# The whole attention in 64-row matmuls that run in pairs on the two halves of the array

## The chip, the cores and the metric

The kernel runs on one core of one Trainium2 chip. The metric is the device time of one execution in microseconds, the median over the runs shown. TensorE (PE) does the matmuls and, in rows marked PEld, loads their weights; VectorE (DVE), ScalarE (ACT) and GpSimd (POOL) do the elementwise work; SyncE (SP) issues nearly all transfers.

## The reference

Three layers follow one another on u, v of shape (4, 3072, 256) and z of shape (4, 3072, 64), in fp32:

```python
scores = (1.0 / S) * np.matmul(z, z.transpose(0, 2, 1))      # S = 3072, 64 columns of z
attn = np.maximum(scores, 0.0) ** 2
x = u * np.matmul(attn, v)                                   # attention
k = np.maximum(xk @ w_k, 0.0); r = sigmoid(xr @ w_r)         # channel mix, xk and xr mix x with x shifted by a row
x = r * (k * k @ w_v)
out = np.maximum(x @ w_in, 0.0) ** 2 @ w_out                 # mlp, 256 -> 2048 -> 256
```

## The kernel before, in words

Every fp32 value is held as two fp32r parts, a high part and a low part (`hi` and `lo`: `lo` is the value minus `hi`), and a product is the sum of hi by hi, lo by hi and hi by lo. So an ordinary product costs three matmuls of 128 rows by 128 columns by 512 columns of moving data.

**Order.** All instructions stand in program order on each engine (`tc.manual_schedule()`, line 823): first `attention`, then `channel_mix`, then `mlp`. Each engine works its own list strictly in that order.

**Attention.** There are 4 batches of 6 blocks (`NBLK` = 24), each block holding 512 rows of the output, transposed (two halves d = 0, 1 of 128 features). A block is made of 24 chunks (`NJ`) of 128 keys; one chunk is one step `s` of the loop in lines 493 to 502. In a step the things planned for it in `todo` come first (loads, the preparation of z, v and u, conversions of weights, the gate of the block before), then `scores` of a chunk that lies up to 7 steps ahead (`LEAD`), then `attend` of chunk s.

`scores` (lines 340 to 361) computes a tile of 128 keys by 512 rows. The scores of a batch are symmetric, so a tile below the diagonal (`g < ib`) is not computed: it was turned on DVE when its mirror image was made (`turn`, line 318), stored to DRAM, and is read back (`load_turned_scores`, line 329), after which ACT makes `hi` (line 346) and DVE `lo` (line 347). Block `ib` of a batch therefore computes 24 - 4 ib chunks and reads 4 ib. For a computed chunk, z with its 64 columns fills the 128 rows of the array with two parts: `zhl` holds hi in rows 0 to 63 and lo in rows 64 to 127, `zlh` the other way round. Two matmuls of 128 rows (lines 351 and 352) give all four products hi·hi + lo·lo and lo·hi + hi·lo. ACT then does relu from PSUM (line 162) and square (line 163), ACT or DVE makes `hi` (lines 356 and 358), DVE turns it where needed (line 322) and makes `lo` (line 361). The score banks are four (`ps_w`), one for each chunk.

`attend` (lines 370 to 383) adds a chunk into the two accumulators of the block (d = 0, 1) with six matmuls: v hi by hi and v lo by hi for each d (lines 379 and 380), then v hi by lo for each d (line 383). The accumulators of odd and even blocks are different banks (`ps_a`, `ps_v`), two each, so eight banks are in use with the four of the scores.

`gate` (lines 385 to 389) is planned for the first step of the next block: for each d one DVE multiplication of the accumulator (in PSUM) by u, then a transfer to DRAM.

**The channel mix of block 0** (`up1` and `down1`, eight times six matmuls each) is spread over steps of the last attention block (lines 474 to 478); the rest, for blocks 1 to 23, is in `channel_mix`.

## Time and profile before

| | |
|---|---|
| median of 3 runs | 2537.62 us (2537.33 to 2539.25) |
| profiled execution | 2538.36 us, span of its instructions 2536.6 us |
| PE busy | 2513.0 us (99%), 11040 matmuls |
| PEld busy | 2072.7 us (82%), 11040 weight loads |
| DVE, ACT, POOL busy | 2007.8 (79%), 1664.6 (66%), 0.2 us (0%) |
| mean granted TensorE clock | 0.998 |

The page of the profile gives the share of the span in which each engine was busy, the chain of work that ended last, and groups of instructions by source line. The views by window give the same for a stretch of the span; timelines list instructions in order, with the idle time before them in square brackets and what released them. A matmul's duration there (0.39 us) is from its start until its result stands, and the next one starts before that; the distance of two starts is what it costs.

### The profile page before, as it was taken

How to read it: one execution, taken by the hardware profiler on the slowest of the kernel's cores; microseconds unless marked ns; L12 is line 12 of the kernel's file. 1: busy time of each engine (PE TensorE's matmuls, PEld its weight loads, DVE VectorE, ACT ScalarE, POOL GpSimd, SP SyncE). 2: the span in 40 equal slices, each digit the busy share in tenths (PEclk: the TensorE clock that was granted, in tenths of full speed). 3: DMA queues.
4: the chain of work that ended last, by engine and by line, in shares of the span. 5: the costliest groups of instructions: out<-in, count | busy, mean ns of one | idle time of the engine just before them, and what ended most of it. 6: DMA issues, size and time to landing. Idle time of an engine off the chain costs nothing.

```text
span 2536.6 us, 31670 instructions
## 1 busy us (share of the span) xinstructions
PE 2513.0 (99%) x11040; PEld 2072.7 (82%) x11040; DVE 2007.8 (79%) x3382; ACT 1664.6 (66%) x2879; POOL 0.2 (0%) x4
## 2 busy tenths in 40 slices
PE   7999999999999999999999999999999999999998
PEld 5888888888888888888888888788888888888887
DVE  8898988988988986777776677877777777777776
ACT  8766876786687654555555566666666666666665
POOL 0000000000000000000000000000000000000000
PEclk9999999999999999999999999999999999999999
DMA  7678677787886770111111112100110011100101
GB/s 189 173 201 202 195 200 186 201 229 185 198 232 185 211 188 26 58 59 42 59 34 50 47 54 67 28 23 17 34 34 17 17 34 34 26 26 17 34 17 17
DMA packets 311121, 243.79 MB, mean 96 GB/s; under 512 B 211377, under 2 KB 229809, under 8 KB 307889
## 3 DMA queue, kind: packets, MB, share of 16 engines
q1 hardware_dynamic: 308848, 241.25, 35.6%
q8 instruction: 86, 1.41, 0.2%
q10 hardware_dynamic: 2112, 0.52, 0.1%
q14 instruction: 75, 0.61, 0.1%
HBM read 136.86 MB, written 104.86 MB: 95 GB/s over the span
## 4 chain that ended last, share of the span: by engine, by line
PE 92%; DVE 3%; ACT 2%; DMA 1%; issue 1%; SPq 1%; DVEq 0%; ACTq 0%
PE ups L652 16%; PE ups L208 13%; PE v L379 9%; PE v L383 9%; PE v L380 9%; PE v L668 6%; PE v L669 6%; PE v L670 6%; PE v L234 3%; PE v L230 3%; PE v L231 3%; PE sps L352 3%; PE sps L351 3%; DMA mixed<-turned 1%; ACT s L692 0%
## 5 line engine op out<-in xcount | busy, mean ns | idle before, releaser
L380 PE MATMUL v<-ahi,vhl 128*128 128x512 f32 x1152 | 448.8, 390 | 2.6 <-DVE vhl L286 2.6
L379 PE MATMUL v<-ahi,vhl 128*128 128x512 f32 x1152 | 449.1, 390 | 1.1 <-ACT ahi L346 1.1
L689 ACT ACTIVATE s<-s 128x512 f32<-128x512 f32 x288 | 181.2, 629 | 333.5 <-DVE s L684 333.4
L383 PE MATMUL v<-alo,vhl 128*128 128x512 f32 x1152 | 356.1, 390 | 4.0 <-DVE alo L361 3.9
L163 ACT ACTIVATE a<-a 128x512 f32<-128x512 f32 x528 | 333.9, 632 | 16.8
L652 PE MATMUL ups<-d,win 128*128 128x512 f32 x1152 | 323.7, 389 | 0.0
L668 PE MATMUL v<-hhi,wout 128*128 128x512 f32 x768 | 299.3, 390 | 0.7 <-ACT hhi L697 0.6
L670 PE MATMUL v<-hlo,wout 128*128 128x512 f32 x768 | 299.3, 390 | 0.5 <-DVE hlo L703 0.5
L669 PE MATMUL v<-hhi,wout 128*128 128x512 f32 x768 | 298.8, 389 | 0.0
L208 PE MATMUL ups<-mixed,wk 128*128 128x512 f32 x1152 | 291.8, 389 | 0.0
L703 DVE TENSOR_TENSOR hlo<-s,hhi 128x512 fp32r<-128x512 f32 x384 | 264.6, 689 | 21.7 <-ACT hhi L697 9.5
L162 ACT ACTIVATE a<-ups 128x512 f32<-128x512 f32 x192 | 114.8, 598 | 235.9 <-PE ups L208 207.9
L383 PEld LDWEIGHTS v<-alo,vhl 128*128 128x128 f32 x1152 | 215.5, 188 | 52.3 <-DVE alo L361 7.9
L380 PEld LDWEIGHTS v<-ahi,vhl 128*128 128x128 f32 x1152 | 216.6, 188 | 48.3 <-DVE vhl L286 3.4
L379 PEld LDWEIGHTS v<-ahi,vhl 128*128 128x128 f32 x1152 | 216.7, 188 | 47.1 <-ACT ahi L346 2.0
L652 PEld LDWEIGHTS ups<-d,win 128*128 128x128 f32 x1152 | 216.3, 188 | 44.9
L208 PEld LDWEIGHTS ups<-mixed,wk 128*128 128x128 f32 x1152 | 216.2, 188 | 44.9
L162 ACT ACTIVATE a<-sps 128x512 f32<-128x512 f32 x336 | 199.2, 593 | 81.5 <-PE sps L352 73.7
L652 PE MATMUL ups<-b,win 128*128 128x512 f32 x864 | 242.9, 389 | 0.0
L692 ACT ACTIVATE s<-s 128x512 f32<-128x512 f32 x384 | 231.2, 627 | 6.1
L322 DVE STREAM_TRANSPOSE turn<-a 128x512 f32<-128x512 f32 x240 | 207.2, 864 | 18.3 <-ACT a L163 16.8
L361 DVE TENSOR_TENSOR alo<-a,ahi 128x512 fp32r<-128x512 f32 x336 | 220.3, 660 | 0.0
(103 smaller groups left out, 3918.0 us busy)
## 6 DMA issues: line engine op xcount, KB each, us to landing
turned<-turn SPq DMA_DIRECT2D x60, 1024.0 KB, 5.1
mixed<-turned SPq DMA_DIRECT2D x220, 256.0 KB, 5.4
raw<-in_v_dram SPq DMA_DIRECT2D x24, 512.0 KB, 4.7
u<-in_u_dram SPq DMA_DIRECT2D x192, 64.0 KB, 4.3
xT<-uT SPq DMA_DIRECT2D x48, 256.0 KB, 2.2
x2d<-xo SPq DMA_DIRECT2D x48, 256.0 KB, 2.2
x<-x2d SPq DMA_DIRECT2D x12, 1024.0 KB, 4.8
out_dram<-y SPq DMA_DIRECT2D x92, 128.0 KB, 2.9
```

The source lines that it names most:

```text
L162: nc.scalar.activation(out=a, in_=ps, func=AF.Relu, scale=scale)
L163: nc.scalar.activation(out=a, in_=a, func=AF.Square)
L208: nc.tensor.matmul(ps, lhsT=lhs(h, c, f), rhs=rhs[:, m, c, :], start=k == 0, stop=k == 3 * ND - 1)
L379: nc.tensor.matmul(acc[n][d], lhsT=vt[:, 0, c, ds_], rhs=hi, start=first, stop=False)
L380: nc.tensor.matmul(acc[n][d], lhsT=vt[:, 1, c, ds_], rhs=hi, start=False, stop=False)
L383: nc.tensor.matmul(acc[n][d], lhsT=vt[:, 0, c, ds_], rhs=lo, start=False, stop=last)
L652: nc.tensor.matmul(ps, lhsT=win[q][:, h, r, w], rhs=x(y), start=first and m == 0, stop=m == 2, skip_group_check=not first)
L668: nc.tensor.matmul(acc[p, b][d], lhsT=w[:, 0, c, ds_], rhs=hi, start=first, stop=False)
L669: nc.tensor.matmul(acc[p, b][d], lhsT=w[:, 1, c, ds_], rhs=hi, start=False, stop=False)
L670: nc.tensor.matmul(acc[p, b][d], lhsT=w[:, 0, c, ds_], rhs=lo, start=False, stop=last)
L692: nc.scalar.activation(out=tmp[g, c], in_=tmp[g, c], func=AF.Square)
L703: nc.vector.tensor_tensor(out=lo, in0=tmp.pop((g, c)), in1=hi, op=ALU.subtract)
```

## The change

In the attention every matmul of 128 rows becomes two of 64 rows, one on rows 0 to 63 and one on rows 64 to 127 of the array, issued one right after the other into PSUM banks of their own.

- Scores are made for two chunks at once (at an even chunk): three products hi·lo, hi·hi, lo·hi of 64 rows each, chunk c on the upper half of the rows and chunk c + 1 on the lower. The product lo·lo is not computed any more. Two banks hold the pair (`ps_s`); both relus are issued together, square and the rest follow chunk by chunk.
- In `attend` each product of 128 keys becomes two of 64 keys, into two accumulators. A block has four accumulators; those of d = 0 exist twice (`bufs=2`, four banks), those of d = 1 once (two banks).
- At the end of a block `gate` adds the halves: for each d an ACT copy of the second half out of PSUM, then for d = 0 a DVE addition from PSUM, for d = 1 a DVE copy of the first half out of PSUM and a POOL addition; the multiplication by u is POOL's.
- At the start of a block the order is: chunk 0 for d = 0, chunk 1 for d = 0, then chunk 0 for d = 1, then chunk 1 for d = 1.
- The channel mix of block 0 is taken out of the last attention block and done at the start of `channel_mix`, whose PSUM pools are now opened after the attention.

```diff
-    ps_v = ctx.enter_context(tc.tile_pool(name="ps_v", bufs=1, space=PSUM))
-    ps_a = ctx.enter_context(tc.tile_pool(name="ps_a", bufs=1, space=PSUM))
-    ps_w = ctx.enter_context(tc.tile_pool(name="ps_w", bufs=4, space=PSUM))
...
+    HALVES = slice(0, P // 2), slice(P // 2, P)
...
+            ps_s = st.enter_context(tc.tile_pool(name="ps_s", bufs=2, space=PSUM))
+            ps_d = [st.enter_context(tc.tile_pool(name=f"ps_{d}", bufs=ND - d, space=PSUM)) for d in range(ND)]
...
-                cs = slice(c * P, (c + 1) * P)
-                ps = ps_w.tile([P, T], F32, tag="w", name="sps")
-                nc.tensor.matmul(ps, lhsT=zhl[b, g][:, cs], rhs=zhl[b, ib], start=True, stop=False)
-                nc.tensor.matmul(ps, lhsT=zlh[b, g][:, cs], rhs=zhl[b, ib], start=False, stop=True)
-                a = relu2(ps, 1.0 / S)
+                if c % 2 == 0:
+                    ps = [ps_s.tile([P, T], F32, tag="w", name="sps") for _ in HALVES]
+                    for k in range(3):
+                        for i, rows in enumerate(HALVES):
+                            top, low = (zlh, zhl) if i else (zhl, zlh)
+                            nc.tensor.matmul(ps[i], lhsT=(low, top, top)[k][b, g][rows, (c + i) * P:(c + i + 1) * P],
+                                             rhs=(top, low, top)[k][b, ib][rows], start=k == 0, stop=k == 2)
+                    for i in range(2):
+                        rel[s + i] = t = el.tile([P, T], F32, tag="a", name="a")
+                        nc.scalar.activation(out=t, in_=ps[i], func=AF.Relu, scale=1.0 / S)
+                a = rel.pop(s)
+                nc.scalar.activation(out=a, in_=a, func=AF.Square)
...
-            def attend(s):
+            def attend(s, d, terms):
+
                 n, b, ib, g, c = chunk(s)
                 first, last = s % NJ == 0, s % NJ == NJ - 1
-                if first:
-                    acc[n] = acc_tiles(ps_a if n % 2 else ps_v)
-                hi, lo = at.pop(s)
-                vt = vhl[b, g]
-                for d in range(ND):
-                    ds_ = slice(d * P, (d + 1) * P)
-                    nc.tensor.matmul(acc[n][d], lhsT=vt[:, 0, c, ds_], rhs=hi, start=first, stop=False)
-                    nc.tensor.matmul(acc[n][d], lhsT=vt[:, 1, c, ds_], rhs=hi, start=False, stop=False)
-                for d in range(ND):
-                    ds_ = slice(d * P, (d + 1) * P)
-                    nc.tensor.matmul(acc[n][d], lhsT=vt[:, 0, c, ds_], rhs=lo, start=False, stop=last)
+                if first and terms[0] == 0:
+                    acc[n, d] = [ps_d[d].tile([P, T], F32, tag=f"r{i}", name=f"v{d}") for i in range(2)]
+                vt, ds_ = vhl[b, g], slice(d * P, (d + 1) * P)
+                for k in terms:
+                    for i, rows in enumerate(HALVES):
+                        nc.tensor.matmul(acc[n, d][i], lhsT=vt[rows, k % 2, c, ds_], rhs=at[s][k // 2][rows],
+                                         start=first and k == 0, stop=last and k == 2)
 
             def gate(n, d):
                 b, t0 = n // NB, (n % NB) * T
-                o = uT.pop((n, d))
-                nc.vector.tensor_tensor(out=o, in0=acc[n][d], in1=o, op=ALU.mult)
+                o, halves = uT.pop((n, d)), acc.pop((n, d))
+                part = x_tile[:, d, 0:T] if n < NBLK - 2 else pools["cv"].tile([P, T], F32, tag="em"[d], name="part")
+                nc.scalar.copy(part, halves[1])
+                if d == 0:
+                    nc.vector.tensor_tensor(out=part, in0=halves[0], in1=part, op=ALU.add)
+                else:
+                    rest = io.tile([P, T], F32, tag="rest", name="rest", bufs=1)
+                    nc.vector.tensor_copy(rest, halves[0])
+                    nc.gpsimd.tensor_tensor(out=part, in0=rest, in1=part, op=ALU.add)
+                nc.gpsimd.tensor_tensor(out=o, in0=part, in1=o, op=ALU.mult)
                 nc.sync.dma_start(out=xT[b][d * P:(d + 1) * P, t0:t0 + T], in_=o)
...
-            units = [(up1, 0), (up1, 1)]
-            for f in range(NF1):
-                units += [(down1, f)] + [(up1, f + 2)] * (f + 2 < NF1)
-            for i, (unit, f) in enumerate(units):
-                at_step(s + 4 + i * 20 // len(units), unit, 0, f)
-
...
+                second = s >= 0 and s % NJ == 1
+                if second:
+                    attend(s, 0, range(3))
+                    attend(s - 1, 1, range(3))
+                    at.pop(s - 1)
                 while made < min(n_steps, s + 1 + min(LEAD, FIRST + max(0, s - 2 * NJ) // NJ)):
                     scores(made)
                     made += 1
-                if 0 <= s < n_steps:
-                    attend(s)
+                if not 0 <= s < n_steps:
+                    continue
+                if second:
+                    attend(s, 1, range(3))
+                elif s % NJ in (0, NJ - 1):
+                    attend(s, 0, range(3))
+                    if s % NJ:
+                        attend(s, 1, range(3))
+                else:
+                    for d, terms in ((0, (0, 1)), (1, (0, 1)), (0, (2,)), (1, (2,))):
+                        attend(s, d, terms)
+                if s % NJ:
+                    at.pop(s)
...
-        gate_r(0, 0)
-        gate_v(0, 0)
-        gate_r(0, 1)
-        gate_v(0, 1)
-        order = [(n, f) for n in range(1, NBLK) for f in range(NF1)]
+        for d in range(ND):
+            gate_r(0, d)
+        order = [(n, f) for n in range(NBLK) for f in range(NF1)]
...
+        for name, bufs in (("ps_v", 1), ("ps_a", 1), ("ps", 4)):
+            pools[name] = ctx.enter_context(tc.tile_pool(name=name, bufs=bufs, space=PSUM, reuse_waits="tile"))
```

## Rows read from the trace of the kernel before

**Rows 1.** First part of the page: busy time of each engine.

```profile
PE 2513.0 (99%) x11040; PEld 2072.7 (82%) x11040; DVE 2007.8 (79%) x3382; ACT 1664.6 (66%) x2879; POOL 0.2 (0%) x4
```

**Rows 2.** Chain of waits that ended last, shares of the span by engine.

```profile
PE 92%; DVE 3%; ACT 2%; DMA 1%; issue 1%; SPq 1%; DVEq 0%; ACTq 0%
```

**Rows 3.** Windows: busy us (count) of PE, PEld, DVE, ACT, POOL; clock; DMA.

```profile
1030.00:1530.00 500.00, 500.00 (x2207) 414.01 (x2207) 368.26 (x647) 284.28 (x467) 0.00 (x0) 1.00 0.14 49
```

**Rows 4.** Groups by line, 0 to 981 us: busy us, mean ns, idle before.

```profile
L379 PE MATMUL v<-ahi,vhl 128*128 128x512 f32 x1152 | 449.1, 390 | 1.1 <-ACT ahi L346 1.1
L352 PE MATMUL sps<-zz 128*128 128x512 f32 x336 | 132.2, 393 | 0.0
L208 PE MATMUL ups<-mixed,wk 128*128 128x512 f32 x48 | 12.2, 389 | 0.0
```

**Rows 5.** Timeline of weight loads and matmuls after an idle stretch of PE.

```profile
245.06 0.19 PEld L379 LDWEIGHTS v<-ahi,vhl 128*128 128x128 f32 x1 [1.08 <-ACT ahi L346]
245.06 0.50 PE L379 MATMUL v<-ahi,vhl 128*128 128x512 f32 x1 [0.66 <-ACT ahi L346]
245.17 0.19 PEld L380 LDWEIGHTS v<-ahi,vhl 128*128 128x128 f32 x1
245.40 0.39 PE L380 MATMUL v<-ahi,vhl 128*128 128x512 f32 x1
...
245.63 0.40 PE L379 MATMUL v<-ahi,vhl 128*128 128x512 f32 x1
```

**Rows 6.** Windows: block 0, then blocks 6, 7, 10 and 11.

```profile
12.00:65.20 53.20, 46.60 (x186) 34.77 (x185) 48.58 (x84) 46.48 (x81) 0.00 (x0) 0.97 0.79 204
259.70:301.40 41.70, 41.70 (x185) 34.55 (x184) 39.54 (x72) 37.18 (x65) 0.00 (x0) 1.00 0.85 240
301.40:341.30 39.90, 39.90 (x177) 33.04 (x176) 33.29 (x60) 31.03 (x53) 0.00 (x0) 1.00 0.68 191
419.30:457.40 38.10, 38.10 (x170) 31.56 (x169) 33.98 (x62) 24.08 (x42) 0.00 (x0) 1.00 0.82 198
457.40:493.60 36.20, 36.20 (x161) 30.00 (x160) 30.36 (x52) 24.23 (x44) 0.00 (x0) 1.00 0.82 212
```

**Rows 7.** Groups by line, 0 to 981 us: instructions nearest to the new gate's.

```profile
L162 ACT ACTIVATE a<-sps 128x512 f32<-128x512 f32 x336 | 199.2, 593 | 81.5 <-PE sps L352 73.7 <-DVE alo L361 4.7 <-DVE uT L298 2.2
L358 DVE CAST ahi<-a 128x512 fp32r<-128x512 f32 x184 | 77.2, 420 | 38.6 <-ACT a L163 37.5
L388 DVE TENSOR_TENSOR uT<-v,uT 128x512 f32<-128x512 f32 x48 | 30.8, 684 | 14.9 <-PE v L383 14.8
```

**Rows 8.** Line 388 (the gate): what DVE waited for before it, us and times.

```profile
  PE v L383: 14.8, 9
```

**Rows 9.** Timeline of DVE: gate of block 7.

```profile
341.28 1.29 DVE L388 TENSOR_TENSOR uT<-v,uT 128x512 f32<-128x512 f32 x2 [1.60 <-PE v L383]
```

**Rows 10.** Timeline: first matmuls of blocks 11 and 12, gates of blocks 10 and 11.

```profile
457.36 0.39 PE L379 MATMUL v<-ahi,vhl 128*128 128x512 f32 x1
462.55 1.29 DVE L388 TENSOR_TENSOR uT<-v,uT 128x512 f32<-128x512 f32 x2
493.62 0.39 PE L379 MATMUL v<-ahi,vhl 128*128 128x512 f32 x1
498.18 1.28 DVE L388 TENSOR_TENSOR uT<-v,uT 128x512 f32<-128x512 f32 x2
```

**Rows 11.** Waits of ACT, 15 to 980 us: total us, times, longest.

```profile
ACT ahi L346 <- DMA mixed<-turned: 31.8, 6, 6.0
```

More of the change, by code (lines that the diff above doesn't have):

```diff
@@ L195, in mix, with acc_tiles @@
         split(store[n][:, 0, c, :], store[n][:, 1, c, :], xm)
-    def acc_tiles(pool=ps_v):
+    HALVES = slice(0, P // 2), slice(P // 2, P)
+    def acc_tiles(pool):
         return [pool.tile([P, T], F32, tag=f"v{d}", name=f"v{d}") for d in range(ND)]
@@ L225, in down1 @@
         if f == 0:
-            acc_v[n] = acc_tiles(ps_a if n % 2 else ps_v)
+            acc_v[n] = acc_tiles(pools["ps_a" if n % 2 else "ps_v"])
         hi, lo = kt.pop((n, f))
@@ L247, in attention @@
             FIRST, LEAD = 4, 7
-            pools["ps"], pools["hidden"] = ps_w, (io, "a", LEAD + 1)
+            pools["hidden"] = (io, "a", LEAD + 1)
+            ps_s = st.enter_context(tc.tile_pool(name="ps_s", bufs=2, space=PSUM))
+            ps_d = [st.enter_context(tc.tile_pool(name=f"ps_{d}", bufs=ND - d, space=PSUM)) for d in range(ND)]
             z_raw, zT, zz, zhl, zlh, vhl, uT = {}, {}, {}, {}, {}, {}, {}
@@ L298, in prep_u @@
                 nc.vector.transpose(uT[n, d], raws.pop(("u", n, d)))
-            at, acc, ready, staged, late = {}, {}, {}, {}, []
+            at, acc, ready, staged, rel, late = {}, {}, {}, {}, {}, []
             def chunk(s):
@@ L552, in channel_mix @@
                 up1(*order[i + lead])
-            if f in (3, 5):
+            if n and f in (3, 5):
                 gate_r(n, (f - 3) // 2)
@@ L648, in product @@
             if first:
-                banks[g, bank] = ps_w.tile([P, T], F32, tag="w", name="ups")
+                banks[g, bank] = pools["ps"].tile([P, T], F32, tag="w", name="ups")
             ps = banks[g, bank]
@@ L662, in down2 @@
             if i == 0 and k in (0, 2):
-                acc[p, b] = acc_tiles((ps_a, ps_v)[b])
+                acc[p, b] = acc_tiles(pools[("ps_a", "ps_v")[b]])
             hi, lo = gt[g, tile_]
```

## The prediction

> **What bounds the kernel now.** I read the page's busy times first: PE is busy 99% of the span, DVE 79%, ACT 66%, POOL not at all [rows 1]. The chain of waits agrees: PE carries 92% of it [rows 2]. So time is won where PE gets less to do, and lost where PE is made to wait. The next view is the price of a matmul. Its row says 390 ns, but that is start to result; in a window without idle time PE starts 2207 matmuls in 500.0 us, so one costs 500.0/2207 = 0.2265 us, at a granted clock of 1.00 (the 2.4 GHz level) [rows 3]. The groups by line count the attention: lines 379, 380 and 383 have 1152 matmuls each, lines 351 and 352 have 336 each [rows 4], so 3456 + 672 = 4128, or 935 us of the first 981.
>
> The last question is how much room the other engines have. Block by block, DVE is busy 39.5 of 41.7 us where all 24 chunks are computed (block 6) and 30.4 of 36.2 where only four are (block 11) [rows 6]: PE is first, but DVE stands close behind it.
>
> **The change, part by part.**
>
> **Scores.** Before, two chunks cost 2 × 2 matmuls of 128 rows. After, three pairs of 64-row matmuls. If a pair costs what a full matmul costs, 672 become 504, and PE saves 168 × 0.2265 = **38.0 us**.
>
> **Attend.** 3456 matmuls become 3456 pairs: no gain, and all of the risk. With the scores there are 3960 pairs, so each ns on a pair costs 3.96 us. No row shows two 64-row matmuls side by side. The nearest row is PE's restart after an idle stretch: a weight load at 245.06, the next at 245.17 with a matmul between, so a load and a start take 0.11 us when nothing else holds them; then matmuls start 0.23 us apart [rows 5]. Two loads and two starts thus fit into 0.22 us, just under 0.2265. That row bounds a pair from below, at 0.22 us (a gain of at most 3960 × 0.0065 = 26 us more). From above: two loads of 0.19 us that don't overlap make 0.38 us (+608 us), two matmuls that don't overlap make 0.453 us (+897 us). I take 0.2265, because it is nearest to the only row on issue, 0.22, and each half streams the 512 columns that a full matmul streams.
>
> **Moved: the channel mix of block 0.** Its 48 + 48 matmuls (line 208 shows the first 48 [rows 4]) go from the attention to the start of the channel mix. PE is the bound on both sides, so 96 × 0.2265 = 21.7 us change places and cost nothing. Their ACT and DVE work moves to where DVE is busy 368 of 500 us [rows 3]; that room hides it.
>
> **Gate, where the others are on time.** ACT gets 48 copies out of PSUM, priced by its relu from PSUM at 593 ns, 1.2 us per block; block 6 leaves it 4.5 us [rows 6, 7]. DVE trades its second multiplication (684 ns) for a copy out of PSUM, between 420 ns (a copy in SBUF) and 684 [rows 7]; I take 684, because that row also reads PSUM. POOL gets 72 operations and has no row for one; nobody on PE's path waits for POOL while it ends before u's buffer is needed ten steps later, some 13 us. SP's transfer of x waits for POOL now, and the loads of turned scores queue behind it; ACT already waited 31.8 us for such loads, six times [rows 11]. A delay of one POOL step, at DVE's 0.68, would make 4 us of that if no buffer hid it; I take nothing and keep 0 to 4.
>
> What PE waits for is the one pair of banks of d = 1. After its last product for d = 0, PE does three pairs for d = 1 and six for d = 0 of the next block before it needs these banks: 9 × 0.2265 = 2.04 us. In that time come an ACT copy (0.59), the DVE addition (0.68) and the DVE copy (0.68): 1.95 us. It fits, just. I put 0.2 us for each of some 14 such ends: **+2.8 us**.
>
> **Gate, where DVE is late.** That sum holds only if DVE has nothing left to do when a block ends. The row of line 388 says how often: DVE waited for PE before the gate 9 times in 24 [rows 8], as in block 7 [rows 9]. The timeline shows the other kind: block 11 starts on PE at 457.36 and block 10's gate at 462.55; block 12 starts at 493.62, block 11's gate at 498.18 [rows 10]. DVE is 5.2 and 4.6 us behind. I find this at the ends of blocks 4, 5, 10, 11, 16 and 17, two per batch, where the next batch's z and v are prepared. Before, it costs nothing, because the next block has other banks. Now PE stands until DVE has copied. At the end of block 11: 4.56 late, + 1.28 for DVE's two operations, - 1.36 for PE's six pairs, + 0.59 if the ACT copy stands in front, is 5.1 us. Does it count at both ends? I take it once per batch: between the two ends the chain also runs through late transfers [rows 11], so the lateness at the second is mostly what was carried over from the first. In such a stretch PE's own saving is lost too: 19 chunks (8 of block 4, 4 of block 5, 7 made ahead) at 0.113 us are 2.1 us. So 3 × (5.1 + 2.1) = **+21.6 us**.
>
> **Score banks** fall from four to two, so a pair of scores waits for both relus of the pair before. Between the pairs PE has 12 pairs of attend, 2.7 us, ACT needs 2 × 0.59; a lateness over 1.5 us makes PE wait. ACT is that late where DVE is, so this moves part of the 21.6 us into the block and adds nothing. If it added, block 0 and the late blocks would show it.
>
> **Block 0** takes 53.2 us with PE busy 46.6: DVE's 48.6 set it [rows 6]. Its share of the saving, 12 × 0.2265, doesn't arrive: **+2.7 us**.
>
> **Sum:** -38.0 + 2.8 + 21.6 + 2.7 = **-10.9 us**. The profiled execution took 2538.4 us (span 2536.6), 0.7 above the median; so 2527.5, and **2526.8 us** against the median of 2537.6.
>
> **The rivals.**
>
> *All of the saving arrives.* If DVE makes up its lateness before the block ends, since its total per batch stays under PE's, only block 0 keeps its share: -38.0 + 2.7, 2502 us. For it: DVE has idle time even in block 11 (5.8 us of 36.2) [rows 6]. Against it: that idle time lies before the burst that ends in the gate.
>
> *The bank of d = 1 decides (other side).* If the lateness builds up anew for each of the six ends, each costs 5.1 to 6 plus about 1 of lost saving: 6 × 6.4 = 38 us in place of 21.6, and with DVE slowed a little by POOL the same. Result 2526.8 + 17 = 2544 us. It decides from a loss of 6 us per late end. For it: the gate stands in DVE's own order, behind everything. SBUF — State Buffer of the Trainium skill, § Who interferes with whom, says that DVE and GpSimd share a port pair that one of them holds for a whole instruction. By it POOL's 72 operations could hold DVE for up to 72 × 0.68 = 49 us, a third of that in late stretches: an estimate of 16 us more, no run here showing any of it.
>
> *A pair costs more than a matmul (other side).* If the second half's load and start follow the first's and each adds what a full matmul adds to its 512 columns at 2.4 GHz (226.5 - 213.3 = 13 ns), a pair takes 2 × (110 + 13) = 246 ns, and 3960 × 0.0195 = 77 us are added: 2604 us. It decides from 10.9/3.96 = 2.8 ns per pair. TensorE: Matmul & The Clock Gate of the Trainium skill, § Measured speedup vs the span model, puts some 4 ns on each further tile of a pack. By that, 16 us come on top, 2543 us; the page times single packs, and no row here shows a stream of them.
>
> *The halves don't run together.* Then the change doesn't do what it says, and 3960 × 0.2265 = 897 us are added: 3424 us. Against it: loads already run under matmuls [rows 5].
>
> **How the numbers follow.** Chances: forecast 0.35, whole saving 0.17, bank of d = 1 0.20, dearer pairs 0.20, no overlap 0.08. A measurement can tell about 0.2%, 5 us, from no change: under 2532.5 is faster, over 2542.7 slower. Faster: 0.17 + 0.31 of the forecast's 0.35, 0.48. Same: 0.04 of the forecast + 0.08 of the bank's, 0.12. Slower: 0.12 + 0.20 + 0.08, 0.40. The range goes from 2499 (the whole saving, a little faster pairs) to 2592 (the nearer part of the dearer pairs); it leaves out no overlap (0.08), the dearest pairs (0.08) and a little below. The forecast alone would be 2514 to 2537.
>
> **What would show it.** Right: PE's weight loads at 7920 in the attention; starts of like halves 0.2265 us apart in block 8; the attention's end near 948 us (981 - 21.7 - 11); at the ends of blocks 4, 5, 10, 11, 16 and 17 PE idle for some us in all, released by DVE's copy. Wrong: starts of like halves 0.23 us or more apart throughout; PE idle before pairs of scores, released by ACT, in blocks that are on time now; a granted clock under 1.00 in the attention; DVE's subtractions longer while POOL runs.

## The result, and the profile after

The changed kernel takes **2563.57 us** (median of 4 runs, 2562.04 to 2565.3), the kernel before 2537.47 beside it: a ratio of 1.0102 (95% interval 1.0085 to 1.012), 26.1 us slower. The forecast was 2526.8, faster; to a slower kernel the prediction gave a chance of 0.40. The measured time lies inside the range, on its other side.

The page of the kernel after; its rows answer to [rows 1] and [rows 2]:

```profile
PE 2501.6 (98%) x14832; PEld 2069.8 (81%) x14832; DVE 2058.1 (80%) x3382; ACT 1654.2 (65%) x2927; POOL 102.0 (4%) x76
PE 65%; DVE 3%; ACT 2%; issue 1%; DMA 1%; DVEq 0%; ACTq 0%; SPq 0%
```

PE's busy time fell by 11 us and not by 38; DVE's grew by 50, though it has 3382 instructions as before. The chain of waits can't be compared: its shares add up to 72% of the span here and to 100% before, since it is followed back only to 713.9 us, so PE's 65% against 92% says nothing. The attention, with 21.7 us of work taken out of it, ends at 985.2 us (forecast: near 948); it ended at 980.6.

What PE waited for in the attention of the kernel after (total us, times, longest):

```profile
PE v L387 <- DVE rest L399: 29.8, 19, 3.5
PE sps L355 <- ACT a L359: 16.6, 12, 4.6
PE sps L355 <- DVE zz L276: 6.8, 1, 6.8
```

The first row is DVE's copy that empties the single bank pair of d = 1, late at 19 of the 23 block ends that another block follows. The second is the pair of score banks. The third is the start of the kernel, which was there before with 7.6 us. The other waits of before, 7.6 us in all, are gone.

Groups by line of the kernel after, 0 to 1010 us (busy us, mean ns, idle before); L359 and L399 answer to lines 162 and 388 of [rows 7]:

```profile
L387 PE MATMUL v<-ahi,vhl 64*128 64x512 f32 x4608 | 664.6, 391 | 29.8 <-DVE rest L399 29.8
L348 DVE TENSOR_TENSOR alo<-mixed,ahi 128x512 fp32r<-128x512 f32 x220 | 171.7, 798 | 28.0 <-ACT ahi L347 17.1 <-DMA u<-in_u_dram 6.9 <-PE v L387 3.9
L401 POOL TENSOR_TENSOR uT<-x,uT 128x512 f32<-128x512 f32 x44 | 62.6, 1424 | 822.6 <-DVE x L396 718.8 <-DMA zn<-in_z_dram 67.2 <-DMA w_out<-m 34.9
L359 ACT ACTIVATE a<-sps 128x512 f32<-128x512 f32 x336 | 187.5, 594 | 116.3 <-PE sps L355 83.0 <-DVE alo L369 28.4 <-PE v L387 3.3
L394 ACT COPY x<-v 128x512 f32<-128x512 f32 x44 | 24.8, 589 | 13.7 <-PE v L387 12.3
L399 DVE COPY rest<-v 128x512 f32<-128x512 f32 x24 | 16.4, 684 | 0.0
```

The gate's copies cost what was assumed (589 and 684 ns). A POOL operation takes 1424 ns, not DVE's 684. DVE's subtraction for turned scores takes 798 ns; the kernel before has the same operation, in this row of the same view:

```profile
L347 DVE TENSOR_TENSOR alo<-mixed,ahi 128x512 fp32r<-128x512 f32 x220 | 146.7, 685 | 32.0 <-ACT ahi L346 30.8 <-DMA u<-in_u_dram 1.0
```

And ACT's relus now wait 28.4 us for DVE's `lo` (line 369), which frees the relu's buffer; before, that was 4.7 us [rows 7].

Timeline around the end of block 10 (start, us, engine, line, operation; idle before it in brackets); it answers to [rows 10]:

```profile
470.73 1.07 ACT L394 COPY x<-v 128x512 f32<-128x512 f32 x2
...
472.42 0.69 DVE L396 TENSOR_TENSOR x<-v,x 128x512 f32<-128x512 f32 x1
473.02 0.68 DVE L399 COPY rest<-v 128x512 f32<-128x512 f32 x1
473.19 1.28 POOL L401 TENSOR_TENSOR uT<-x,uT 128x512 f32<-128x512 f32 x1 [40.26 <-DVE x L396]
473.62 5.18 DVE L348 TENSOR_TENSOR alo<-mixed,ahi 128x512 fp32r<-128x512 f32 x4
473.76 0.73 PE L387 MATMUL v<-ahi,vhl 64*128 64x512 f32 x4 [3.48 <-DVE rest L399]
...
475.66 1.92 PE L387 MATMUL v<-ahi,vhl 64*128 64x512 f32 x8
...
478.20 1.07 PE L387 MATMUL v<-ahi,vhl 64*128 64x512 f32 x8
```

ACT has copied at 471.8. DVE still has older work and copies at 473.02, and PE stands for 3.48 us. Then DVE's next four subtractions take 5.18 us while POOL runs its three operations. And PE, once released, does eight matmuls in 1.92 us that take 1.07 a little later.

Windows of the kernel after around that wait (length, then busy us and count of PE, PEld, DVE, ACT, POOL; granted clock; DMA share, GB/s):

```profile
470.20:473.76 3.56, 0.08 (x2) 0.00 (x1) 3.52 (x7) 2.12 (x5) 0.57 (x1) 1.00 0.65 184
473.76:477.30 3.54, 3.54 (x20) 2.89 (x22) 3.54 (x3) 1.24 (x2) 3.46 (x3) 0.64 0.56 196
500.00:503.60 3.60, 3.60 (x36) 2.98 (x34) 3.60 (x8) 3.53 (x8) 0.00 (x0) 1.00 0.44 134
```

PE starts 10 pairs in the 3.54 us behind the wait, at a granted clock of 0.64, and 18 in 3.60 us where it did not wait, at 1.00. So this wait is followed by a stretch in which a pair costs up to 0.43 us, at the 1.2 GHz level. The same is seen at 215, 270, 714, 754 and 952 us, behind waits of 1.5 to 3.5 us, and not at every wait: behind 2.27 us at 513 us the clock stays at 1.00.

Adding up, over the whole attention, by how much the distance from one matmul (or pair) to the next exceeds 0.2265 us gives the time PE lost there: 15.7 us before, 80.9 after. The difference, 65.2, less the 38.0 saved, is 27.2; the two profiled spans differ by 26.9. So the rest of the kernel changes next to nothing, and the question is where the 65 us come from.

### The profile page after: what moved, and what is told of

Read it like the earlier page. It is cut to its first block, busy times and chain, and to the rows that moved or that the text cites. A ratio compares the mean times of both kernels' runs of the same rounds, so it can differ in the third digit from the quotient of the medians.

```text
span 2563.5 us, 39587 instructions
## 1 busy us (share of the span) xinstructions
PE 2501.6 (98%) x14832; PEld 2069.8 (81%) x14832; DVE 2058.1 (80%) x3382; ACT 1654.2 (65%) x2927; POOL 102.0 (4%) x76
## 4 chain that ended last, share of the span: by engine, by line
PE 65%; DVE 3%; ACT 2%; issue 1%; DMA 1%; DVEq 0%; ACTq 0%; SPq 0%
PE ups L673 16%; PE ups L207 13%; PE v L387 7%; PE v L689 6%; PE v L690 6%; PE v L691 6%; PE v L230 3%; PE v L233 3%; PE v L229 3%; PE sps L355 1%; ACT s L713 0%; ACT s L710 0%; DVE hlo L724 0%; DVE s L705 0%; DVE alo L369 0%
## 5 line engine op out<-in xcount | busy, mean ns | idle before, releaser
L387 PE MATMUL v<-ahi,vhl 64*128 64x512 f32 x4608 | 664.6, 391 | 29.8 <-DVE rest L399 29.8
L387 PEld LDWEIGHTS v<-ahi,vhl 64*128 64x128 f32 x4608 | 470.5, 187 | 117.6 <-DVE rest L399 39.0
L387 PE MATMUL v<-alo,vhl 64*128 64x512 f32 x2304 | 400.3, 390 | 0.1
L724 DVE TENSOR_TENSOR hlo<-s,hhi 128x512 fp32r<-128x512 f32 x384 | 264.7, 689 | 21.7 <-ACT hhi L718 8.7
L387 PEld LDWEIGHTS v<-alo,vhl 64*128 64x128 f32 x2304 | 245.7, 186 | 41.8 <-DVE alo L369 1.8
L359 ACT ACTIVATE a<-sps 128x512 f32<-128x512 f32 x336 | 187.5, 594 | 116.3 <-PE sps L355 83.0
L361 ACT ACTIVATE a<-a 128x512 f32<-128x512 f32 x336 | 204.0, 630 | 0.2
L347 ACT CAST ahi<-mixed 128x512 fp32r<-128x512 f32 x220 | 129.0, 618 | 115.8 <-PE v L387 67.8
L86 DVE CAST hhi<-a 128x512 fp32r<-128x512 f32 x192 | 81.6, 425 | 142.2 <-ACT a L160 140.1
```

The costliest lines, as they stand in the source:

```text
L359: nc.scalar.activation(out=t, in_=ps[i], func=AF.Relu, scale=1.0 / S)
L361: nc.scalar.activation(out=a, in_=a, func=AF.Square)
L387: nc.tensor.matmul(acc[n, d][i], lhsT=vt[rows, k % 2, c, ds_], rhs=at[s][k // 2][rows], start=first and k == 0, stop=last and k == 2)
L724: nc.vector.tensor_tensor(out=lo, in0=tmp.pop((g, c)), in1=hi, op=ALU.subtract)
```

## Experiments: the matmuls themselves

**The move of block 0's channel mix alone**, in the kernel before:

```diff
-            units = [(up1, 0), (up1, 1)]
...
-        order = [(n, f) for n in range(1, NBLK) for f in range(NF1)]
+        order = [(n, f) for n in range(NBLK) for f in range(NF1)]
```

> The kernel before with block 0's channel mix moved behind the attention and nothing else changed. Theory A (PE is the bound on both sides, the move costs nothing): within 3 us of before. Theory B (the start of the channel mix waits for its first results, and the attention's last block gains nothing): 4 to 10 us slower.

2538.33 us, ratio 0.9997 (0.9988 to 1.0007). The move costs nothing, as forecast.

**Pairs for the scores alone**; attend with 128 rows, gate and banks as before (the edit against the changed kernel):

```diff
-                for k in terms:
-                    for i, rows in enumerate(HALVES):
-                        nc.tensor.matmul(acc[n, d][i], lhsT=vt[rows, k % 2, c, ds_], rhs=at[s][k // 2][rows], ...
+                nc.tensor.matmul(acc[n][d], lhsT=vt[:, 0, c, ds_], rhs=hi, start=first, stop=False)
...
```

> Only the scores in pairs of 64 rows, attend in whole matmuls of 128 rows with the accumulators, the gate and the order of before; four score banks (two pairs). PE changes between 64 and 128 rows 2 x 168 times. Theory A (such a change costs no more than the next matmul): PE saves its 38 us, nothing waits for a bank, 2500 to 2512. Theory B (each change empties the array first; the one change at the attention's end in the changed kernel shows PE idle for 0.35 us): 336 x 0.1 to 0.35 us = 34 to 118 us come on top, 2536 to 2620, with idle time of PE before the first score pair and before the first attend after it.

2571.63 us, ratio 1.0128 (1.0111 to 1.0145): the part that should have saved 38 us costs 33. PE's waits are small here. The time is in the matmuls themselves, as PE's timeline of this kernel shows:

```profile
511.27 0.61 PE L391 MATMUL v<-alo,vhl 128*128 128x512 f32 x2
511.81 0.97 PE L355 MATMUL sps<-zz 64*128 64x512 f32 x6
512.71 0.50 PE L387 MATMUL v<-ahi,vhl 128*128 128x512 f32 x1
513.05 0.40 PE L388 MATMUL v<-ahi,vhl 128*128 128x512 f32 x1
513.28 0.39 PE L387 MATMUL v<-ahi,vhl 128*128 128x512 f32 x1
```

From the first start to 513.05 are two matmuls, three pairs and one matmul, 6 × 0.2265 = 1.36 us at full rate; they take 1.78. The two changes between 128 and 64 rows cost 0.21 us each. There are 331 such changes in the trace, 66.7 us over the full rate in all; everywhere else PE loses 20.6 us, 4.9 more than before. -38.0 + 66.7 + 4.9 is 33.6, and 32.8 were measured. TensorEngine Tiling (Array Packing) of the Trainium skill, § Key Properties, says that changing the tiling mode drains TensorE; the trace agrees as far as it can show it: it has a loss of 0.2 us at each change, not what happens inside the engine. Such a loss at each change is why the change had to take attend along.

**Scores of four chunks at a time**, so that there are half as many changes (the edit against the run before):

```diff
-                if c % 2 == 0:
-                    ps = [ps_s.tile([P, T], F32, tag="w", name="sps") for _ in HALVES]
+                if c % 4 == 0:
+                    for j in range(4):
+                        banks[s + j] = ps_s.tile([P, T], F32, tag="w", name="sps")
...
```

> Scores alone in pairs of 64 rows, attend whole, as in the run with scores only, but four chunks' scores are made at once into all four score banks: half as many changes between 64 and 128 rows. In the run with scores only each change cost 0.2 us (starts 0.42 to 0.43 us apart in place of 0.2265). Theory A (the price is per change): 166 x 0.2 = 33 us less than 2571.6, 2536 to 2544. Theory B (all four banks taken at once make PE wait for ACT's relus): 2550 or more, with PE idle before scores, released by ACT.

2544.5 us, 1.0019 (1.0009 to 1.0028): 27 us less. The price is one per change: the median change costs 0.204 us in both runs. With 165 changes, half as many, PE loses 36.3 us there, 33.7 of it for the changes at that price and the rest in waits and slow matmuls at a dozen of them. Elsewhere PE loses 10.2 more than before, half of it in one wait of 5.2 us for a score bank at the start: -38.0 + 36.3 + 10.2 = 8.5, against 7.8 of the profiled execution.

**No halves at all, but the new order and banks**: one bank for d = 1, two for d = 0, four for the scores, 128 rows everywhere (the edit against the kernel before):

```diff
+                if first and terms[0] == 0:
+                    acc[n, d] = ps_d[d].tile([P, T], F32, tag="r0", name=f"v{d}")
...
+                nc.vector.tensor_tensor(out=o, in0=acc.pop((n, d)), in1=o, op=ALU.mult)
```

> No halves: whole matmuls in scores and attend, DVE's gate of before, but one bank for d = 1 (two for d = 0), the new order at the start of a block, and block 0's channel mix moved. Nothing is saved on PE. Theory A (the single bank costs little without POOL): 2540 to 2548. Theory B (the single bank behind a late DVE is the main loss): PE waits 4 to 6 us at the ends of blocks 4, 5, 10, 11, 16 and 17, 20 to 35 us in all, 2558 to 2573.

2569.17 us, 1.0118 (1.0103 to 1.0133). Without a single 64-row matmul the loss is there:

```profile
PE v L379 <- DVE uT L385: 21.2, 11, 5.5
```

Here DVE's two multiplications both come before the bank of d = 1 is free, and the loss in the attention is 48.1 us against 15.7: the single bank costs some 32 us by itself, 21.2 of them in that wait and most of the rest in matmuls behind it, of which 32 start 0.40 to 0.45 us after the one before.

## Experiments: the gate

**Without POOL** (what is left out stands in the expectation):

```diff
-                    nc.vector.tensor_tensor(out=part, in0=halves[0], in1=part, op=ALU.add)
+                    nc.vector.tensor_tensor(out=o, in0=halves[0], in1=part, op=ALU.add)
                 else:
-                    rest = io.tile([P, T], F32, tag="rest", name="rest", bufs=1)
-                    nc.vector.tensor_copy(rest, halves[0])
-                    nc.gpsimd.tensor_tensor(out=part, in0=rest, in1=part, op=ALU.add)
-                nc.gpsimd.tensor_tensor(out=o, in0=part, in1=o, op=ALU.mult)
+                    nc.vector.tensor_copy(o, halves[0])
```

> The changed kernel without POOL's three operations per block end: the second half of d = 1 is not added and the multiplication by u is left out; ACT's copies and DVE's two operations stay. Theory A (POOL holds DVE: while POOL runs, DVE's subtractions stretch, 50 us in all, and the late DVE makes PE wait for the banks): DVE busy falls by about 50 us to some 2008, PE's wait for the copy of d = 1 falls from 29.8 to 10 to 20 us, the time to 2530 to 2545. Theory B (the one bank pair of d = 1 behind DVE's own order is enough by itself, POOL does no harm): DVE's wait ends stay, PE's wait stays at 25 to 30 us, the time stays at 2558 to 2566.

2556.95 us, 1.0071 (1.0056 to 1.0086). DVE's busy time falls by 53 us, with the same 3382 instructions, but the time by only 7 to 8 (6.6 between the medians, 8.0 when each is taken against the kernel before beside it), and the wait at the block ends stays:

```profile
PE v L387 <- DVE uT L398: 29.5, 18, 3.5
```

So POOL's 72 operations do hold DVE up, and DVE mostly makes it up before PE notices. SBUF — State Buffer of the Trainium skill, § Who interferes with whom, says that a DVE instruction with both inputs in SBUF contends with a GpSimd instruction that reads SBUF; the trace agrees (798 against 685 ns), and the estimate drawn from it for the rival, 49 us of DVE, came close to the 53 seen, by luck in part: it took 0.68 us for a POOL operation, and one takes 1.42.

**All arithmetic on DVE**, the two that empty banks first, nothing left out:

```diff
+                nc.vector.tensor_tensor(out=part, in0=halves[0], in1=part, op=ALU.add)
...
+                for d, (o, part) in enumerate((summed.pop(n), (o, part))):
+                    nc.vector.tensor_tensor(out=o, in0=part, in1=o, op=ALU.mult)
```

> The changed kernel with the whole gate on ACT and DVE: per block two ACT copies, two DVE additions out of PSUM first, then two DVE multiplications; nothing on POOL. DVE gets 24 x 2 operations more of 0.62 us, 30 us, and loses what POOL took from it. Theory A (POOL took 50 us of DVE): DVE busy about 2038, the time 2540 to 2555, under that of the change. Theory B (POOL does no harm): DVE busy about 2088, the time 2565 to 2590, over that of the change.

2557.64 us, 1.0073 (1.0058 to 1.0088): as without POOL. What matters is not who does the arithmetic but who empties the bank.

**ACT empties both banks of d = 1** and one of d = 0; DVE adds, for d = 0 out of the other bank, and multiplies:

```diff
+                nc.scalar.copy(part[0], p1)
+                nc.scalar.copy(part[1], q1)
+                nc.scalar.copy(rest, q0)
+                nc.vector.tensor_tensor(out=part[0], in0=p0, in1=part[0], op=ALU.add)
+                nc.vector.tensor_tensor(out=part[1], in0=rest, in1=part[1], op=ALU.add)
```

> The changed kernel with another gate: ACT copies both halves of d = 1 and one of d = 0 out of PSUM, DVE adds and multiplies, POOL does nothing. The banks of d = 1 then wait for ACT alone. Theory A (DVE is what is late, ACT reaches the gate earlier, at the end of block 10 by 1.7 us): PE's wait for these banks falls from 26 to 30 us to 10 to 18, the time from 2557.6 (gate on DVE) to 2538 to 2548. Theory B (ACT is as late as DVE, since it waits for DVE's buffers): PE's wait stays over 24 us and the time at 2553 to 2562.

2537.09 us, 0.9997 (0.9987 to 1.0006): 20.5 us less than with all on DVE, and the kernel is level with the one before. The waits of the run with all on DVE, then of this one:

```profile
PE v L387 <- DVE x L397: 25.9, 18, 3.5
PE sps L355 <- ACT a L359: 11.9, 11, 4.0
PE sps L355 <- ACT a L359: 15.2, 11, 4.4
PE v L387 <- ACT rest L400: 10.5, 11, 2.1
```

The wait at the block ends falls by 15.4 us, that before the scores grows by 3.3. Here DVE's place in the gate is shown as the cause of the larger part: each end is set by DVE's lateness as long as DVE empties the bank.

## Experiments: who is late, and why

**Less work for DVE**, in the changed kernel: only three of the eight operations of each conversion of weights are left.

```diff
-        return [start, clamp_low, clamp_high, sign, top, mantissa, bottom, end] + [rest] * rests
+        return [start, top, end] + [rest] * rests
```

> The changed kernel with three of the eight DVE operations of each of the 25 weight conversions (the weights are wrong then); everything else, POOL's part too, as in the change. DVE has some 60 us less to do in the attention. Theory A (the lateness of DVE holds the banks): PE's two waits, 46 us together, fall under 25, the time to 2525 to 2542. Theory B (the place of the gate and the number of banks make PE wait, whatever DVE's load): the waits stay at 38 to 46, the time within 8 us of 2563.6.

2543.23 us, 1.0019 (1.0009 to 1.0028), 20 us less, for 60 us of DVE work taken away; the time is nearest to theory A, and the waits fall less than it said:

```profile
PE v L387 <- DVE rest L399: 22.3, 11, 3.4
PE sps L355 <- ACT a L359: 8.2, 7, 4.2
```

Both waits shrink, the one before the scores by half: that wait, too, goes back to DVE, which holds the relu's buffers and the `hi` and `lo` that follow.

Three runs tried to take the lateness away without taking work away, all on the kernel in which ACT empties the banks: a **fifth relu buffer**, **conversions kept out of blocks 4, 10, 16 and 22**, and **three conversion steps at a time where DVE has most room**.

```diff
-                        rel[s + i] = t = el.tile([P, T], F32, tag="a", name="a")
+                        rel[s + i] = t = (spare if (s + i) % 5 == 4 else el).tile([P, T], F32, tag="a", name="a")
```

> The same with a fifth buffer for the tiles between relu and the split. In the changed kernel ACT waits 28 us for such buffers before its relu, and PE's score pairs wait 12 to 17 us for that relu, since there are only two score banks. Theory A (the buffers are what makes ACT late): PE's waits before score pairs fall under 8 us, the time 5 to 10 us below the run with ACT's drains. Theory B (DVE's pace as such makes ACT late, a buffer more only moves it): within 3 us of that run.

```diff
-            free = [t for t in range(NJ, n_steps - NJ) if chunk(t + later)[3] <= chunk(t + later)[2] < NB - 1]
+            free = [t for t in range(NJ, n_steps - NJ) if chunk(t + later)[3] <= chunk(t + later)[2] < NB - 2]
```

> The run with ACT's drains (2537.1), and the weight conversions kept out of blocks 4, 10, 16 and 22 as well: their 218 steps fall on the blocks 1 to 3 of each batch, more densely. Theory A (PE's waits before scores and at the late ends come from DVE's load in just those blocks): the 9.5 us of waits before scores in blocks 4, 10 and 16 go, with the half-clock stretches behind them; 2520 to 2532. Theory B (the load only moves): DVE becomes late in blocks 2 and 3, 2535 to 2545.

```diff
+                if fg <= fib < NB - 1 and (fib < NB - 2 or fb == B - 1):
+                    free += [t] * (3 if fib == 1 else 1)
```

> The same, but the steps go where DVE has most room: three per step in the second block of each batch, one per step in the first, third and fourth, and in block 22, whose end was on time before. Theory A: 2515 to 2530, at or below the run with conversions kept out evenly, and below the kernel before. Theory B (the preparation of the next batch alone makes DVE late): 2533 or more.

2538.65 us (1.0, 0.999 to 1.0009), 2538.82 (1.0, 0.9991 to 1.001) and 2545.38 (1.0026, 1.0017 to 1.0036). None helps. The fifth buffer is no clean test, since the same edit also draws `rest`, the gate's copy, from the relu's buffers; the last run moves the crowd to where the scores wait, 21.9 us before them in place of 15.2. Shifting DVE's work about did not pay.

## Experiments: the banks

**Two score banks in the kernel before.** The first try drew a second tile for every chunk and never used it:

```diff
                 ps = ps_w.tile([P, T], F32, tag="w", name="sps")
+                ps_w.tile([P, T], F32, tag="w", name="skipped")
```

> The kernel before with only two of its four score banks in use (whole matmuls, everything else as before). Theory A (in the late stretches two banks are too few: ACT's relu comes 2 to 4 us after the matmul, and a bank is wanted again after 3.4 us): PE waits before scores, released by ACT, 10 to 20 us in all, most of it in blocks 0, 4, 10 and 16; 2546 to 2560. Theory B (the waits before scores in the changed kernel come from the halves or the pairing alone): within 3 us of before.

2538.21 us, 0.9996 (0.9987 to 1.0006), but the edit did nothing: an unused tile takes no bank, and in 65 cases a score matmul two chunks later began before the relu had ended, as four banks allow. This run measures nothing. The second try gave the scores a pool of two (with block 0 moved, which costs nothing):

```diff
+            ps_s = st.enter_context(tc.tile_pool(name="ps_s", bufs=2, space=PSUM))
```

> Whole matmuls, the accumulators, gate and order of before, and a score pool of two banks; block 0's channel mix moved (which cost nothing). Theory A (two banks are too few where ACT is late): PE waits before scores, released by ACT, 10 to 25 us in all, most in blocks 0, 4, 10 and 16; 2548 to 2565. Theory B (the pairing makes these waits, since both relus of a pair stand in a row): under 5 us of waits, within 5 us of before.

2542.95 us, 1.0019 (1.001 to 1.0029):

```profile
PE sps L352 <- ACT a L159: 11.1, 12, 3.6
```

Two score banks in place of four cost about 5 us by themselves, with PE no faster than before: 11.1 us of new waits, in place of the 7.6 of before that are gone.

**Only the upper half of the rows in attend**, to have banks for all; what it leaves out stands in the expectation (the edit against the kernel before):

```diff
-                    nc.tensor.matmul(acc[n][d], lhsT=vt[:, 0, c, ds_], rhs=hi, start=first, stop=False)
+                    nc.tensor.matmul(acc[n][d], lhsT=vt[HALVES[0], 0, c, ds_], rhs=hi[HALVES[0]], start=first, stop=False)
```

> Scores in pairs as in the change, attend with the upper 64 rows alone (the lower 64 keys of each chunk are left out of the sum), one bank per accumulator: four score banks and two full sets of accumulators fit, DVE's gate of before. PE issues as many slots of 0.2265 us as the change. Theory A (the shortage of banks took all of the saving): PE waits under 12 us after the start, 2498 to 2508. Theory B (PE, faster, runs into DVE and ACT whatever the banks): waits of 15 us or more, 2512 or more.

3282.6 us, 1.293 (1.2911 to 1.2949), and no answer on the banks, because the matmuls themselves took nearly twice as long. PE's timeline in the attention and at the start of the channel mix, and windows in both:

```profile
601.28 0.62 PE L387 MATMUL v<-ahi,vhl 64*128 64x512 f32 x1
601.71 0.62 PE L388 MATMUL v<-ahi,vhl 64*128 64x512 f32 x1
...
1700.93 5.47 PE L207 MATMUL ups<-mixed,wr 128*128 128x512 f32 x12
1706.22 5.66 PE L207 MATMUL ups<-mixed,wk 128*128 128x512 f32 x24
```

```profile
600.00:700.00 100.00, 100.00 (x268) 76.67 (x266) 52.65 (x83) 38.77 (x69) 0.00 (x0) 1.00 0.37 95
1800.00:2000.00 200.00, 200.00 (x884) 165.62 (x883) 149.04 (x269) 114.65 (x192) 0.00 (x0) 1.00 0.15 51
```

Starts are 0.43 us apart without any wait, and 200/884 = 0.226 in the channel mix. It was not the 64 rows as such: the first 12 matmuls of the channel mix, of 128 rows, still start 0.43 us apart, up to 1706.2 us, and only then 0.23. At just that point the trace's first entry of the granted clock begins, at 1.00; before it the column's 1.00 has no entry behind it. Distance (0.43 us) and duration (0.62) are those of the 1.2 GHz stretches of the kernel after. So the attention most likely ran at the 1.2 GHz level; why the clock did not rise in it stays open.

**Banks enough for pairs**: both halves as in the change, but the upper always adds into d = 0 and the lower into d = 1. What that leaves out stands in the expectation.

```diff
+                for k in (0, 1, 0, 1, 2, 2):
+                    for d, rows in enumerate(HALVES):
+                        nc.tensor.matmul(acc[n][d], lhsT=vt[rows, k % 2, c, d * P:(d + 1) * P], rhs=(hi, lo)[k // 2][rows],
+                                         start=first and k == 0 and not started, stop=last and k == 2 and ended)
```

> The changed kernel with the same number of pairs in scores and attention, but no bank shared between two blocks that follow each other: rows 0 to 63 always add into the bank of d = 0, rows 64 to 127 always into that of d = 1, each pair twice over, so the six pairs per chunk stay (it leaves out the other half of the keys for each d and counts the rest double). That frees four banks: two sets of accumulators, four score banks, and the gate of the kernel before on DVE alone; order within a block as before, block 0's channel mix moved. Theory A (the shortage of banks took the saving): the waits at block ends and before scores go, and the 38 us of 168 products come to 25 to 38: 2500 to 2513 us, ratio 0.985 to 0.990, with under 20 us of idle PE time in the attention. Theory B (PE that runs faster only waits for DVE's and ACT's preparation of the scores, whatever the banks): the waits before scores stay or move to the products that need hi or lo, and the time is 2515 to 2540, ratio 0.991 to 1.001.

2514.71 us, 0.9907 (0.989 to 0.9923), **23.3 us under the kernel before**. Waits of PE in the attention, and a window of it:

```profile
PE v L388 <- DVE alo L369: 8.2, 13, 1.6
PE sps L355 <- DVE zz L276: 6.7, 1, 6.7
PE v L388 <- DVE vhl L287: 2.7, 1, 2.7
PE v L388 <- ACT ahi L347: 2.7, 3, 1.8
```

```profile
830.00:930.00 100.00, 100.00 (x886) 82.65 (x884) 88.95 (x156) 57.06 (x101) 0.00 (x0) 1.00 0.74 196
```

886 half matmuls in 100 us are 443 pairs at 0.226 us: a pair costs what a full matmul costs, as forecast. The waits at block ends and before scores are gone. The time lies between the two ranges, 2 us above the theory of the banks and at the edge of its rival: 31.2 us are lost in the attention, 15.5 more than before. Five of these are the start, about ten are short waits for `lo`, `hi` and v, where a faster PE meets DVE. So the shortage of banks, with the gate that it forces, is the larger cause, some 49 us between this run and the change (2563.6 - 2514.7), and a PE that runs into DVE the smaller. This kernel is no version to keep.

## Experiments: a better version

More `hi` on ACT, to relieve DVE, in the kernel in which ACT empties the banks; first with the conversions moved as above, then without:

```diff
-                if g > ib and s % 3 < 2:
+                if ib or g > ib and s % 3 < 2:
```

> The run with conversions earlier (2538.8), and the high part of every computed tile made by ACT in blocks 1 to 5 of a batch, so that DVE has some 34 copies less per batch, 12 us. Theory A (DVE's pace is what PE still waits for): 2522 to 2533. Theory B (ACT, which gets the work, becomes the late one): 2536 or more.

> The same step on the run with ACT's drains (2537.1), conversions where they were. Theory A: the waits before scores in blocks 4, 10 and 16 fall from 9.5 us to under 5, 2523 to 2533. Theory B: 2536 or more.

2538.09 us (1.0, 0.999 to 1.0009) and 2534.21 (0.9986, 0.9977 to 0.9996). The second gains a little. On it, the banks of d = 1 got more time by order alone:

```diff
-                nc.scalar.copy(part[0], p1)
                 nc.scalar.copy(part[1], q1)
                 nc.scalar.copy(rest, q0)
+                nc.scalar.copy(part[0], p1)
...
-                    attend(s, 0, range(3))
                     if s % NJ:
                         attend(s, 1, range(3))
+                    attend(s, 0, range(3))
```

> The complete kernel with ACT emptying three of the four banks and making more of the high parts (2534.2 us), with two changes of order at the block's end only: the last chunk multiplies d = 1 before d = 0, which gives the single set of banks of d = 1 three more pairs, 0.68 us, and ACT empties these two banks before it copies for d = 0, 0.59 us sooner. Theory A (what is left of the loss is the wait for the single set, 14.8 us in 10 ends of about 1.35 us, with matmuls at half the clock behind them): each end loses its 0.59 + 0.68 us of wait, some 10 to 13 us in all; 2520 to 2526 us, ratio 0.993 to 0.995, and PE's waits for the copies of d = 1 under 3 us. Theory B (PE that runs faster waits for the preparation of the scores in their place): the waits before scores and for low parts grow by what the ends lose, and the time stays at 2530 to 2536, ratio 0.997 to 0.999.

**2531.91 us**, 0.9975 (0.9965 to 0.9985): 6.5 us under the kernel before, the fastest complete version found. The waits of the run with more `hi` on ACT, then of this one:

```profile
PE sps L355 <- ACT a L359: 12.8, 14, 4.3
PE v L387 <- ACT rest L400: 10.5, 10, 1.7
```

```profile
PE sps L355 <- ACT a L359: 16.1, 15, 4.2
PE v L387 <- ACT rest L399: 5.5, 10, 1.2
```

The ends lose 5 us of wait, the scores get 3.3 back: what the rival theory expected. With two score banks left, time won at the block ends goes to the next scarce bank. Not tried: halves that swap between banks of d = 0 and d = 1, which would need no sum.

## Why the prediction was wrong, point by point

The time that PE lost in the attention, from its matmuls as above, by where it was lost (us); "attend" holds the block ends. The times are medians, the losses are those of the profiled execution:

| kernel | time over before | first 70 us | scores | attend | sum |
|---|---|---|---|---|---|
| before | 0 | 13.3 | 0.1 | 2.3 | 15.7 |
| the change | +26.1 | 18.1 | 14.4 | 48.4 | 80.9 |
| without POOL | +18.1 | 17.8 | 9.6 | 46.2 | 73.6 |
| less work for DVE | +4.9 | 17.8 | 4.9 | 38.0 | 60.6 |
| ACT empties the banks | -1.3 | 17.9 | 12.3 | 22.1 | 52.4 |
| fastest complete version | -6.5 | 17.7 | 17.6 | 12.5 | 47.8 |
| banks enough | -23.3 | 18.2 | 2.1 | 10.9 | 31.2 |

**Right.** The saving of 38.0 us and the price of a pair, 0.2265: the run with banks enough shows both, and the rivals of dearer pairs and of halves that don't run together fall. TensorE: Matmul & The Clock Gate of the Trainium skill, § Measured speedup vs the span model, puts some 4 ns on each further tile; in a stream of pairs the traces show no such addition (443 pairs in 100 us with banks enough). Moving block 0 costs nothing. The lateness at the ends of blocks 4, 5, 10, 11, 16 and 17 is where it was named: these six have 2.3, 3.6, 4.0, 2.5, 4.3 and 3.3 us of gap, the slower first matmuls behind it included, 20.0 in all.

**"It fits, just. I put 0.2 us for each of some 14 such ends": +2.8 forecast, 17.4 measured.** This step failed most. Of the 37.4 us in gaps over 0.6 us between products of attend, the six late ends make 20.0 and the others, 13 of them, 17.4, or 1.3 us each. The sum of 1.95 against 2.04 us assumed DVE idle at a block's end and left 0.09 us to spare. The row that the prediction read says otherwise: DVE waited for PE at 9 of 24 gates [rows 8], and of the other 15 only six were taken as late. In the kernel before, DVE came to the gate with work in hand at the ends of blocks 6, 12 and 18 too, 1.1 us after the last product for d = 0. The end of block 6 there (that product is the first of the two):

```profile
300.50 0.61 PE L383 MATMUL v<-alo,vhl 128*128 128x512 f32 x2
302.04 1.28 DVE L388 TENSOR_TENSOR uT<-v,uT 128x512 f32<-128x512 f32 x2
```

The timeline of the kernel after at the same end, which was held to be on time, shows what DVE does there:

```profile
312.11 1.08 ACT L394 COPY x<-v 128x512 f32<-128x512 f32 x2
312.25 0.43 DVE L366 CAST ahi<-a 128x512 fp32r<-128x512 f32 x1 [0.50 <-ACT a L361]
312.59 0.69 DVE L369 TENSOR_TENSOR alo<-a,ahi 128x512 fp32r<-128x512 f32 x1
...
313.20 0.69 DVE L396 TENSOR_TENSOR x<-v,x 128x512 f32<-128x512 f32 x1
313.80 0.68 DVE L399 COPY rest<-v 128x512 f32<-128x512 f32 x1
...
314.53 0.73 PE L387 MATMUL v<-ahi,vhl 64*128 64x512 f32 x4 [1.24 <-DVE rest L399]
```

ACT's two copies are done in time. DVE still waits 0.50 us for a chunk's square, then makes its `hi` and its `lo`, which stand ahead of the gate in its order, and only then adds and copies: PE waits 1.24 us. In the kernel after, DVE's addition starts 0.7 to 2.9 us after the last product for d = 0 at all 17 ends that were held to be on time; of this, ACT's copy in front of it takes 0.6.

**"I take it once per batch": 15.3 us forecast, 20.0 measured.** It builds up anew at both ends, as the rival said, but to 3.3 us on average and not 5.1. DVE is less late there: its addition starts 2.5 to 4.2 us after the last product for d = 0, where the gate of before started 5.1 to 6.7 us after it. In four of these six blocks PE has already waited before scores; whether that is the reason stays open.

**"This moves part of the 21.6 us into the block and adds nothing": 10.7 us measured** in gaps before scores after the start. All lie in late stretches, at 215 to 257, 445 to 461 and 685 to 701 us. The 21.6 us held 6.3 for PE's saving lost in these stretches; ends and scores together are 30.7. ACT's relus wait for buffers that DVE frees (28.4 us against 4.7), so DVE's lateness reaches the score banks by another way than the gate. With less work for DVE, the time lost before scores falls from 14.4 to 4.9 us, which bears this out. That two banks cost 5 us even with a PE that is no faster was measured by itself; what the other half comes from, the faster PE, the pairing or a later DVE, was not separated.

**What had no term.** The slower matmuls behind a wait: some 50 pairs start 0.40 to 0.45 us after the one before, 9 to 10 us. The prediction listed a granted clock under 1.00 as a sign of being wrong and gave it no price. The first 70 us lost 4.8 us more than before and not 2.7, in every kernel with pairs in scores and attend; why stays open.

**POOL** was put at nothing, with 0 to 4 us kept for transfers. It cost DVE 53 us, and the time 7 to 8.

So the forecast's losses, 2.8 + 21.6 + 2.7 = 27.1 us, were 65.2: ends 37.4, scores 10.7, start 4.8, together 52.9, and the rest mostly slow matmuls. The rival that the bank of d = 1 decides named the place and the side; its 2544 us was too small, most of all by the ends that it held to be on time.

## What to carry to other kernels

A buffer of which there is only one set is priced by what the engine that empties it still has in its queue, not by the operations that empty it: count the lateness at every turn, and let the least loaded engine do the emptying, first in its order. Here, with PE the bound at 99%, a second engine at 80% had no room for new duties on PE's path; see what a faster PE would wait for next before its saving is counted, and add the slow matmuls that can follow a wait. Don't mix matmuls of 64 and 128 rows in a fine pattern: on this kernel that took back nearly twice what the halves saved.

## What the runs showed of the hardware that was not expected

- Each change between matmuls of 128 and of 64 rows cost 0.2 us, in either direction, so 331 changes cost 67 us and 165 about 34.
- Two 64-row matmuls on the two halves, in a stream, cost 0.226 us together, loads included, the same as one of 128 rows.
- Behind six of the waits in the kernel after, of 1.5 to 3.5 us each, the granted clock fell to the 1.2 GHz level; behind the one at 474 us it was 0.64 on average over 3.54 us, with pairs up to 0.43 us apart.
- With the upper half alone in use in attend, matmuls started 0.43 us apart for the whole attention; those of 128 rows behind it did so too until 1706.2 us, where the first entry of the granted clock begins, and then 0.23 us apart.
- 72 operations on POOL, of 1.4 us each, lengthened DVE's work by 53 us: four subtractions took 5.18 us beside POOL, against 685 ns for one without it.
